# The middle pair of token tiles forms its second product by Strassen's scheme too

## The chip, the cores and the metric

The kernel runs on one core of a Trainium2 chip. The metric is the device time of one execution in microseconds (us): the median of three runs of the kernel before is 820.15 us (819.52 to 820.28). TensorE is the matrix engine, VectorE, ScalarE and GpSimd work on tiles, and SyncE (SP) only issues transfers. In the rows they are PE, DVE, ACT, POOL and SP.

## The reference

Attention within chunks of 64 tokens is followed by a feed-forward layer with softplus, all in float32:

```
scores = scale * q_c @ k_c^T        # per chunk of 64 tokens, head size 64, 8 heads, batch 8
attn   = exp(scores - max) / (sum + 1e-09)
x      = (attn @ v_c), heads side by side         # 4608 tokens x 512
h      = x @ w_in                                  # 512 -> 2048
g      = maximum(h, 0) + log1p(exp(-abs(h)))       # softplus
out    = g @ w_out                                 # 2048 -> 512, 4608 x 512
```

## The kernel before

The 4608 tokens are nine tiles of 512. Every float32 operand of the two large products is split into a high part (rounded to the type that TensorE takes) and a low part (the rest), and each product is formed by three matmuls: high by high, high by low, low by high.

The first three tiles are formed plainly (`gemm1`, `gemm2`). The other six are three pairs, and the first product of each pair (x by w_in) is formed by Strassen's scheme: seven block products in place of eight. The blocks' sums of w_in ("weight images", seven for each of eight column groups j) are made once, written to DRAM (`scratch`) and loaded again for every pair into a ring of SBUF tiles (`ring_load`, from GpSimd's queue). For each j, `product` issues seven groups of six matmuls, `hold` and `mix` combine them, `soft` applies softplus. In the first and the middle pair, the second tile's softplus results are spilled to DRAM and loaded again (`spill_store`, `spill_load`); the second product (g by w_out) is plain: `gemm2`, 12 matmuls for each of 16 chunks and each tile. In the last pair the second product is Strassen's too (`sum_product`: seven products k, eight blocks j, six matmuls each). For this its own weight images are made from w_out on VectorE and ScalarE: `v_total` (L902), `v_sum` (L915) and `v_lo` (L923), stored by `v_store` from SP's queue, half of them during the middle pair and half during the last; `image_load` (L930) brings a whole half image (1 MB). The left operand's block differences are `t_sum` (L937), and their high and low parts `g_hi` (L960) and `g_lo` (L964). `combine` (L999) adds the block results, `out_turn` (L1010) transposes them and `out_store` (L1024) writes them.

Attention for later tiles runs in bursts between the products: a burst is two halves, each 32 small matmul records for attn @ v (L661) and 32 for the scores (L557). Nine bursts lie beside the plain tiles, four beside the first pair and four beside the middle pair (three in its first product, one in its second).

The order of the work is not written by hand. Each step is a task with a cost, its needs and an urgency; `Plan.order` lists the tasks on each engine by a model of these costs, and TensorE's order is a written list (`seq`). Once listed, each engine runs its own list in order and waits on the others by semaphores; a transfer in a queue stands behind all that was issued there before. The constants at the end of the kernel (`IN_SUPER`, `QUEUE`, `V_DVE` and the like) set places, queues and engines.

Of the kernel before, what the change touches and what calls it, by code (L numbers as in the profile page):

```python
# [192 lines left out]
def chunked_attention_softplus_ffn(  # L193
# [42 lines left out]
    xpool = ctx.enter_context(tc.tile_pool(name="xpool", bufs=2))  # L236
    ld = ctx.enter_context(tc.tile_pool(name="ld", bufs=1))
# [13 lines left out]
    sp.tile([P, G_PAD], F32, name="pad", bufs=1)  # L251
# [37 lines left out]
    BOTH = (2,)  # L289
# [3 lines left out]
    def raw_tile(n, new=False):  # L293
        if new or ("raw tile", n) not in live:
            live["raw tile", n] = ld.tile([P, 2 * UW + 16], I32, name=f"raw{n}")
        return live["raw tile", n][:, : 2 * UW].bitcast(F32)
# [314 lines left out]
    def att_max(i):  # L611
        scs = live["sc", i]
        n = scs[0].shape[1]
        mx = att.tile([P, n * len(scs), scs[0].shape[2]], F32, name="mx", bufs=2)
# [23 lines left out]
    def att_den(i):  # L638
        e = live["e", i]
        den = att.tile([P, e.shape[1], e.shape[2]], F32, name="den", bufs=2)  # L640
# [99 lines left out]
    def w_image(w, k):  # L740
# [3 lines left out]
        return ring_tile(w["s"] in BOTH and w["j"] % 2, k // NX)[:, n * MT : (n + 1) * MT]  # L744

    def ring_tile(other, part):
        if other and "other" not in live:
            live["other"] = [x_tile(0, F32R) for _ in range(2)]
        t = live["other"][part] if other else x_of(FAST - 1)[part]
        return t.rearrange("p s k t -> p (s k t)")  # L750
# [42 lines left out]
    def ring_load(w, part):  # L793
        src = scratch[w["j"]]
        if w["name"] == "0_0" and part == 0:
# [3 lines left out]
        t = ring_tile(w["s"] in BOTH and w["j"] % 2, part).bitcast(F32)  # L799
        cols = slice(NX * MT, 7 * MT) if part else slice(0, NX * MT)  # L800
        on("ring").dma_start(t[:, : cols.stop - cols.start], src[:, cols])  # L801
# [50 lines left out]
    def soft(w, i, j):  # L852
        src = {(0, 0): tmp_of(0), (0, 1): tmp_of(1), (1, 0): w["bank"][0], (1, 1): tmp_of(2)}[i, j]
        if w["s"] in BOTH:
            nc.scalar.activation(u_block(w["j"], i, j), src, AF.Softplus)
            return
# [11 lines left out]
    def u_block(j, i, c):  # L868
        if ("u", j, i, c) not in live:
            n, fc = 2 * i + c, 2 * (j - 2) + i  # L870
            if j == 0:
                t = ends.bitcast(F32)[:, n * MT : (n + 1) * MT]
            elif j == 1:
                t = blk_tile(("eT", "qe")[n // 2])
            elif fc < HALF_FC:
                t = const.tile([P, DM], F32, name=("wo_hi", "wo_lo")[c] + str(fc))
            else:
                t = late_tile(2 * (fc - HALF_FC) + c, F32)
            live["u", j, i, c] = t
        return live["u", j, i, c]  # L880

    SUM_OF = (2, 3, 5, 4)

    def own_image(j, q):
        on("wo").dma_start(images[6, :, j, q, :], wo[2 * j + 1][q].bitcast(F32)[:, HC:])

    def v_space(j):
        at = SUM_AT[j]
        if ("v space", at) not in live:
            if at in SUM_RAW:  # L890
                live["v space", at] = [raw_tile(n, True) for n in range(3)]
            else:
                t = x_raw(1).rearrange("p s k t -> p (s k t)")
                live["v space", at] = [t[:, : 2 * MT], t[:, 2 * MT :]]
        return live["v space", at]

    def v_total(j, b):
        hi, lo = (t.bitcast(F32) for t in wo[2 * j + b])
        space = v_space(j)
        t = space[0]  # L900
# [3 lines left out]
    def v_sum(j, n):  # L904
        if SUM_AT[j] in SUM_RAW:
            t = v_space(j)[n // 2 - 2][:, n % 2 * MT : (n % 2 + 1) * MT]
        else:
            t = v_space(j)[n < 2][:, n % 2 * MT : (n % 2 + 1) * MT]
# [19 lines left out]
    def image_load(k, part):  # L928
        t = ring_tile(k % 2, part).bitcast(F32).rearrange("p (j q c) -> p j q c", q=2, c=HC)
        on("image").dma_start(t, images[k, :, part * FC // 4 : (part + 1) * FC // 4])  # L930

    def t_sum(n, j):
# [4 lines left out]
        (nc.gpsimd if (n, j) in TS_POOL else nc.vector).tensor_tensor(out, a, b, op=ALU.subtract)  # L937
# [4 lines left out]
    def slot_of(k, j):  # L942
        return k + 4 * (j == FC // 2 - 1) if k < 2 else (FC // 2 * k + j + 2) % GI

    def g_image(k, j):
        if ("gi", k, j) not in live:
            n = slot_of(k, j)
            if n >= GI:
                t = [w.rearrange("p a k f -> p (a k f)")[:, (n + 2) * MT : (n + 3) * MT] for w in wi[0]]
            elif k == 6:  # L950
                t = [w.rearrange("p a k f -> p (a k f)")[:, j * MT : (j + 1) * MT] for w in wi[0]]
            elif n < 2:
                t = [sp.tile([P, MT], F32R, name=f"g_{q}", bufs=LAG + 1) for q in ("hi", "lo")]
            else:
                t = [high(n - 1)[:, q * MT : (q + 1) * MT] for q in range(2)]
            live["gi", k, j] = t
        return live["gi", k, j]

    def g_hi(k, j):
        nc.scalar.copy(g_image(k, j)[0], u_block(j, *OF_G[k]))  # L960

    def g_lo(k, j):
        hi, lo = g_image(k, j)
        (nc.gpsimd if (k, j) in GL_POOL else nc.vector).tensor_tensor(  # L964
# [5 lines left out]
    def sum_product(k, j, cts, cols=slice(0, MT)):  # L970
        if k < 2 and j == 0:
            live["acc", k] = [po_tile(2 * k + ct) for ct in range(2)]
        if k > 1:
            w = ring_tile(k % 2, j // (FC // 4)).rearrange("p (j q c) -> p j q c", q=2, c=HC)[:, j % (FC // 4)]
        else:
# [762 lines left out]
```

## Time and profile before

| what | value |
|---|---|
| median of three runs | 820.15 us |
| the profiled execution, from first to last instruction | 819.6 us |
| TensorE busy | 808.6 us, 99% |
| VectorE, ScalarE, GpSimd busy | 67%, 50%, 30% |
| DMA, mean over the span | 151.27 MB, 185 GB/s |
| plain tiles, until about | 312 us |
| first pair: first product, second product | 312 to 435.8, to 484.6 us |
| middle pair: first, second | 484.6 to 608.2, to 656 us |
| last pair: first, second and end | 656 to 754, to 819.6 us |

The profile's durations overlap on TensorE: a matmul is shown from its start to its modelled end, and the next starts before. Busy shares are means over stages with different limits, so the stages are read one by one.

### The profile page before, as it was taken

How to read it: one execution, taken by the hardware profiler on the slowest of the kernel's cores; microseconds unless marked ns; L12 is line 12 of the kernel's file. 1: busy time of each engine (PE TensorE's matmuls, PEld its weight loads, DVE VectorE, ACT ScalarE, POOL GpSimd, SP SyncE). 2: the span in 40 equal slices, each digit the busy share in tenths (PEclk: the TensorE clock that was granted, in tenths of full speed). 3: DMA queues.
4: the chain of work that ended last, by engine and by line, in shares of the span. 5: the costliest groups of instructions: out<-in, count | busy, mean ns of one | idle time of the engine just before them, and what ended most of it. 6: DMA issues, size and time to landing. Idle time of an engine off the chain costs nothing.

```text
span 819.6 us, 15544 instructions
## 1 busy us (share of the span) xinstructions
PE 808.6 (99%) x5719; PEld 668.2 (82%) x5719; DVE 552.9 (67%) x1031; ACT 411.6 (50%) x694; POOL 247.8 (30%) x331
## 2 busy tenths in 40 slices
PE   9999999999999999999999999999999999999997
PEld 7878878888888888878888888888888888888885
DVE  4898985386378668355376877484766738734983
ACT  4767765345344474353445544354643455545451
POOL 1557647787887621320000000000000001000124
PEclk9999999999999999999999999999999999999999
DMA  9986758773675254986667547879775367746464
GB/s 215 250 212 182 185 169 240 217 199 94 137 194 145 49 145 158 214 207 171 210 170 223 132 115 237 255 175 253 217 225 176 116 222 234 252 169 205 126 218 69
DMA packets 200509, 151.27 MB, mean 185 GB/s; under 512 B 157520, under 2 KB 175184, under 8 KB 196208
## 3 DMA queue, kind: packets, MB, share of 16 engines
q1 hardware_dynamic: 186880, 99.89, 45.1%
q0 software_dynamic: 11680, 50.15, 20.8%
q8 instruction: 45, 0.74, 0.4%
q10 hardware_dynamic: 1872, 0.23, 0.2%
q14 instruction: 32, 0.26, 0.1%
HBM read 106.95 MB, written 41.94 MB: 182 GB/s over the span
## 4 chain that ended last, share of the span: by engine, by line
PE 85%; DVE 4%; DMA 4%; SPq 2%; issue 2%; ACT 2%; POOL 1%; POOLq 0%; DVEq 0%; ACTq 0%
PE po L1046 33%; PE pa L832 27%; PE pa L703 13%; PE po L980 8%; PE pa L661 2%; PE pa L557 2%; SPq L392 1%; DMA raw<-in_moe_w_in_dram 1%; DMA xb<-scratch 1%; PE po L413 1%; DMA late<-in_v_dram 1%; POOL out_dram L1024 1%; DVE wib L339 1%; DMA raw<-in_moe_w_out_dram 0%; DVE ka L544 0%
## 5 line engine op out<-in xcount | busy, mean ns | idle before, releaser
L1046 PE MATMUL po<-late,g_hi 128*128 128x512 f32 x420 | 128.9, 392 | 0.0
L801 POOL DMA_DIRECT2D xb<-scratch x39 | 20.9, 535 | 306.5 <-PE pa L832 279.7
L846 DVE TENSOR_TENSOR wib<-wib,pa 128x512 f32<-128x512 f32 x72 | 49.4, 687 | 71.1 <-PE pa L832 63.6
L832 PE MATMUL pa<-wi_hi,xb 128*128 128x512 f32 x304 | 93.6, 389 | 0.0
L1046 PEld LDWEIGHTS po<-late,g_hi 128*128 128x128 f32 x420 | 78.2, 188 | 16.6
L832 PE MATMUL pa<-wib,xb 128*128 128x512 f32 x360 | 87.5, 390 | 0.4 <-DVE wib L846 0.4
L1046 PE MATMUL po<-wo_hi,g_hi 128*128 128x512 f32 x224 | 84.8, 394 | 0.0
L1046 PE MATMUL po<-wo_lo,g_hi 128*128 128x512 f32 x224 | 83.8, 390 | 0.0
L1046 PE MATMUL po<-wo_hi,g_lo 128*128 128x512 f32 x224 | 83.6, 389 | 0.0
L1046 PE MATMUL po<-late,g_lo 128*128 128x512 f32 x224 | 83.3, 389 | 0.0
L832 PEld LDWEIGHTS pa<-wib,xb 128*128 128x128 f32 x360 | 67.4, 188 | 15.2 <-DVE wib L846 0.8
L715 ACT CAST g_hi<-ends 128x512 fp32r<-128x512 f32 x64 | 39.6, 619 | 78.1 <-PE po L1046 63.5
L719 DVE TENSOR_TENSOR g_lo<-ends,g_hi 128x512 fp32r<-128x512 f32 x64 | 44.0, 688 | 48.5 <-ACT g_hi L715 48.2
L711 ACT ACTIVATE u<-pa 128x512 f32<-128x512 f32 (+1 forms) x50 | 29.0, 581 | 82.1 <-PE pa L703 82.0
L838 ACT COPY wib<-pa 128x512 f32<-128x512 f32 x72 | 41.9, 588 | 50.0 <-PE pa L832 49.9
L832 PEld LDWEIGHTS pa<-wi_hi,xb 128*128 128x128 f32 x304 | 57.1, 188 | 11.8
L719 DVE TENSOR_TENSOR g_lo<-u,g_hi 128x512 fp32r<-128x512 f32 (+1 forms) x39 | 28.1, 720 | 53.4 <-ACT g_hi L715 53.1
L857 ACT ACTIVATE ends<-wib 128x512 f32<-128x512 f32 x48 | 30.3, 632 | 59.9 <-DVE wib L846 59.9
L832 PE MATMUL pa<-wi_lo,xb 128*128 128x512 f32 x152 | 59.1, 389 | 0.0
L1046 PEld LDWEIGHTS po<-wo_hi,g_lo 128*128 128x128 f32 x224 | 42.1, 188 | 9.0
L1046 PEld LDWEIGHTS po<-late,g_lo 128*128 128x128 f32 x224 | 42.0, 188 | 8.9
L1046 PEld LDWEIGHTS po<-wo_lo,g_hi 128*128 128x128 f32 x224 | 42.1, 188 | 8.6
(274 smaller groups left out, 1725.2 us busy)
## 6 DMA issues: line engine op xcount, KB each, us to landing
xb<-scratch POOLq DMA_DIRECT2D x19, 1024.0 KB, 6.0
xb<-scratch POOLq DMA_DIRECT2D x20, 768.0 KB, 6.3
raw<-in_moe_w_in_dram SPq DMA_DIRECT2D x16, 512.0 KB, 5.7
raw<-in_moe_w_out_dram SPq DMA_DIRECT2D x16, 512.0 KB, 4.9
scratch<-ends SPq DMA_DIRECT2D x16, 512.0 KB, 3.2
out_dram<-raw SPq DMA_DIRECT2D x28, 256.0 KB, 3.8
spill<-ends SPq DMA_DIRECT2D x14, 512.0 KB, 4.5
ends<-spill SPq DMA_DIRECT2D x14, 512.0 KB, 3.9
```

The lines of the kernel that those rows point to most:

```text
L557: nc.tensor.matmul(pa[c2][o, col : col + C], qT[r, a * HP + hl, :], kT[r, a * HP + hl, :], start=True, stop=True,)
L703: nc.tensor.matmul(ph, wt[:, c, :], x[:, ts_, c, :], start=(n == 0), stop=(n == 3 * KC - 1))
L711: nc.scalar.activation(w["u"], w["ph"], AF.Softplus)
L715: nc.scalar.copy(w["hi"], w["u"])
L719: (nc.gpsimd if pool else nc.vector).tensor_tensor(w["lo"], w["u"], w["hi"].bitcast(F32), op=ALU.subtract)
L801: on("ring").dma_start(t[:, : cols.stop - cols.start], src[:, cols])
L832: nc.tensor.matmul(w["bank"][BANK[k]], wts[:, q, c, :], x[:, c, :], start=k in OPENS and c + n == 0, stop=c == 1 and n == 2, skip_group_ch ...
L838: nc.scalar.copy(tmp_of(n), w["bank"][2 * (n == 2)])
L846: nc.vector.tensor_tensor(to, a, b, op=ALU.add)
L857: nc.scalar.activation(u_tiles(j)[i], src, AF.Softplus)
L980: nc.tensor.matmul(live["acc", ACC[k]][ct][:, cols], (w[:, q] if k > 1 else w[q])[:, ct * P : (ct + 1) * P], g[:, cols], start=k < 3 and j ...
L1046: nc.tensor.matmul(pos[w["m"]][t], terms[n][0][:, j * P : (j + 1) * P], terms[n][1], start=(w["first"] and n == 0), stop=n == 2 and (w["la ...
```

## The change

`BOTH`, the pairs whose second product is Strassen's, becomes `(1, 2)`. All seven weight images of w_out are now in DRAM: the four sums (`add_sums`) are made once, during the first pair, and stored from GpSimd's queue; the three that are plain parts of w_out (`own_image`) are stored beside the plain tiles and in the middle and last pair loaded again (`own_load`), since the tiles that held w_out now hold the softplus results of the pair. Images of even k are loaded one block (256 KB) at a time into tiles of their own, images of odd k by halves into the ring; the ring is loaded in four pieces per block pair instead of two in these two pairs. The last burst moves from the middle pair's second product into its first, and the four bursts of that pair are split around three matmuls. The spill of the middle pair goes away.

```
-    BOTH = (2,)
+    BOTH = (1, 2)
+    FB = BOTH[0]
...
+    def own_load(j, k):
+        on("own").dma_start(wo[FC - 4 + j % 2][k].bitcast(F32), images[k, :, j].rearrange("p q c -> p (q c)"))
+
+    def image_tile(k, j):
+        if k < 2:
+            return wo[FC - 4 + j % 2][k].rearrange("p (q c) -> p q c", q=2)
+        if k % 2:
+            return ring_tile(j // (FC // 4)).rearrange("p (j q c) -> p j q c", q=2, c=HC)[:, j % (FC // 4)]
...
+        return live["even"][j].rearrange("p (q c) -> p q c", q=2)
...
+    def image_load(k, js):
+        if len(js) == 1:
+            on("image").dma_start(image_tile(k, js[0]).bitcast(F32), images[k, :, js[0]])
+            return
...
-        (nc.gpsimd if (n, j) in TS_POOL else nc.vector).tensor_tensor(out, a, b, op=ALU.subtract)
+        (nc.gpsimd if pool else nc.vector).tensor_tensor(out, a, b, op=ALU.subtract)
...
-    IN_SUPER = ([0, 2], [0, 5], [0, 7], [1, 3])
+    IN_SUPER = ((0, 0, 2), (0, 0, 5), (0, 0, 7), (0, 1, 4), (1, 0, 1), (1, 0, 3), (1, 0, 5), (1, 0, 7))
...
-    QUEUE = dict(wd="SP", wo="SP", ring="POOL", us="SP", ul="SP", image="SP", vd="SP")
-    TS_POOL = ()
+    QUEUE = dict(wd="SP", wo="SP", ring="POOL", us="SP", ul="SP", image="SP", vd="POOL", own="SP")
...
-    V_DVE = tuple(range(8))
+    V_DVE = (0, 1, 2, 3, 4, 5, 7)
...
+    PARTS = ((0, 1, 2, 3), (4, 5, 6)), ((0, 1), (2, 3), (4, 5), (6,))
...
-            add_burst(n, 0, j)
+            if n in BOTH and (n, 0, j) in bursts:
+                for i in range(2):
+                    seq += [f"B{tag((n, 0, j))}_{i}"] + fill[i : i + 1]
+                fill = fill[2:]
+            else:
+                add_burst(n, 0, j)
...
                     pool = (t, j) in TS_POOL
-                    plan.add(f"ts{t}_{j}", "POOL" if pool else "DVE", 1.3 if pool else 0.69, partial(t_sum, t, j), needs,
+                    plan.add(f"ts{n}.{t}_{j}", "POOL" if pool else "DVE", 1.3 if pool else 0.69, partial(t_sum, t, j, pool), needs,
...
+    add_sums(FB)
     for n in BOTH:
-        add_sums(n)
+        add_second(n)
```

The new `TS_POOL` begins `((2, 2, 6), (2, 1, 0), ...` and `GL_POOL` likewise.

On TensorE, at a burst in the middle pair's first product, before (L661 and L557 are the burst's two kinds, L1046 the second product):

```order
L1046 MATMUL po_5691<-wo_hi_104,g_lo 128x512
L661 MATMUL pa<-eT,raw_5392 64x64 x16
L557 MATMUL pa<-ka,qe 64x64 x16
L661 MATMUL pa<-eT,raw_5392 64x64 x16
L557 MATMUL pa<-ka,qe 64x64 x16
L1046 MATMUL po_5688<-wo_hi_106,g_hi 128x512
L1046 MATMUL po_5688<-wo_lo_107,g_hi 128x512
```

And after (L665 and L560 are the burst, L1001 `sum_product`, L832 `product`):

```order
L1001 MATMUL po_5903<-g_hi,late_1435 128x512 x2
L1001 MATMUL po_5903<-g_lo,late_1435 128x512
L665 MATMUL pa<-eT,raw_5600 64x64 x16
L560 MATMUL pa<-ka,qe 64x64 x16
L1001 MATMUL po_5982<-g_hi,late_1436 128x512 x2
L1001 MATMUL po_5982<-g_lo,late_1436 128x512
L665 MATMUL pa<-eT,raw_5600 64x64 x16
L560 MATMUL pa<-ka,qe 64x64 x16
L1001 MATMUL po_5983<-g_hi,late_1436 128x512 x2
L1001 MATMUL po_5983<-g_lo,late_1436 128x512
L832 MATMUL pa<-wi_hi,xb 128x512 x2
```

The two halves of the burst no longer touch: three large matmuls stand between them and three behind, and then the next block pair begins.

On GpSimd, in the first pair's first product, before (L801 are the ring loads, L527 a load for attention):

```order
L801 DMA xb<-scratch 128x1536
L801 DMA xb<-scratch 128x2048
L801 DMA xb<-scratch 128x1536
L801 DMA xb<-scratch 128x2048
L801 DMA xb<-scratch 128x1536
```

And after (L930 is `v_store`, L530 a load for attention):

```order
L801 DMA xb<-scratch 128x2048
L930 DMA images<-wib_3919 128x512
L930 DMA images<-u 128x512
L801 DMA xb<-scratch 128x1536
L930 DMA images<-raw_4071 128x512 x2
L930 DMA images<-xa 128x512 x2
L801 DMA xb<-scratch 128x2048
L930 DMA images<-xa 128x512 x2
L801 DMA xb<-scratch 128x1536
L530 DMA raw_4448<-in_q_dram 32x8x32 x8
L801 DMA xb<-scratch 128x2048
```

Between most ring loads there now stand one to four stores of weight sums. Each of them waits for VectorE's last step on its tile, and the ring load waits behind it.

On VectorE, in the middle pair's second product, before (L719 are low parts, L811 and L823 the next pair's x images):

```order
L719 TENSOR_TENSOR g_lo<-ends,g_hi 128x512
L811 TENSOR_TENSOR xa<-xa 128x2x8x64
L719 TENSOR_TENSOR g_lo<-ends,g_hi 128x512
L823 TENSOR_TENSOR wi_lo<-xa,wi_hi 128x1024 x2
L719 TENSOR_TENSOR g_lo<-ends,g_hi 128x512
```

And after (L988 are low parts, L958 block differences):

```order
L988 TENSOR_TENSOR g_lo<-late_6747,g_hi 128x512
L988 TENSOR_TENSOR g_lo<-late_6837,g_hi 128x512
L958 TENSOR_TENSOR ends<-ends 128x512
L988 TENSOR_TENSOR late_1436<-ends,late_1435 128x512
L811 TENSOR_TENSOR xa<-xa 128x2x8x64
L988 TENSOR_TENSOR late_1494<-wo_end,late_1493 128x512
L988 TENSOR_TENSOR g_lo<-wo_lo_6127,g_hi 128x512
L958 TENSOR_TENSOR late_5933<-late_5933,late_5900 128x512
L823 TENSOR_TENSOR wi_lo<-xa,wi_hi 128x1024
```

Two kinds of work on the left operand stand where there was one, and the next pair's images stand among them.

## Rows read from the trace of the kernel before

**Rows 1.** Totals of the page: engine, busy us, share of the span, instructions.
```profile
PE 808.6 (99%) x5719; PEld 668.2 (82%) x5719; DVE 552.9 (67%) x1031; ACT 411.6 (50%) x694; POOL 247.8 (30%) x331
```

**Rows 2.** TensorE's waits, longest first: us in total, times, longest.
```profile
PE po L418 <- POOL ident masks.py:199: 1.4, 1, 1.4
...
PE pa L832 <- DVE wib L846: 0.4, 1, 0.4
```

**Rows 3.** Stages: length, busy us per engine, granted clock, DMA share, GB/s.
```profile
312.00:435.80 123.80, 123.36 (x897) 101.38 (x895) 68.73 (x129) 55.25 (x94) 19.82 (x34) 1.00 0.74 197
435.80:484.60 48.80, 48.80 (x333) 40.37 (x334) 39.52 (x66) 22.15 (x36) 0.00 (x0) 1.00 0.64 170
484.60:608.20 123.60, 123.60 (x901) 102.34 (x900) 83.02 (x167) 61.42 (x110) 8.50 (x16) 1.00 0.77 219
608.20:656.00 47.80, 47.80 (x271) 39.45 (x270) 33.86 (x53) 21.05 (x34) 0.53 (x1) 1.00 0.47 145
656.00:754.00 98.00, 98.00 (x435) 81.12 (x434) 53.70 (x97) 50.48 (x92) 6.90 (x13) 1.00 0.64 215
754.00:811.00 57.00, 57.00 (x253) 47.22 (x252) 47.11 (x74) 27.21 (x48) 15.51 (x24) 1.00 0.53 157
```

**Rows 4.** The chain that ended last: start, us, what.
```profile
374.29 5.44 PE pa L832 x24
...
753.93 48.97 PE po L980 x216
```

**Rows 5.** Timeline of TensorE around a joined burst: start, duration, instruction.
```profile
526.36 0.39 PE L1046 MATMUL po<-wo_hi,g_lo 128*128 128x512 f32 x1
526.68 0.69 PE L661 MATMUL pa<-eT,raw 64*64 64x64 f32 x32
...
531.62 0.62 PE L832 MATMUL pa<-wi_hi,xb 128*128 128x512 f32 x2
```

**Rows 6.** The same around a split burst (36 large matmuls in it).
```profile
117.51 2.93 PE L703 MATMUL pa<-xb,wib 128*128 128x512 f32 x12
120.36 0.69 PE L661 MATMUL pa<-eT,q 64*64 64x64 f32 x32
...
124.41 0.69 PE L661 MATMUL pa<-eT,k 64*64 64x64 f32 x32
...
128.35 0.39 PE L703 MATMUL pa<-xa,wi_hi 128*128 128x512 f32 x1
```

**Rows 7.** Groups on VectorE: busy us, mean ns of one, idle before.
```profile
L823 DVE TENSOR_TENSOR wi_lo<-xa,wi_hi 128x1024 fp32r<-128x1024 f32 x12 | 14.5, 1220 | 1.8 <-ACT wi_hi L818 1.7
L964 DVE TENSOR_TENSOR g_lo<-wo_hi,g_hi 128x512 fp32r<-128x512 f32 x12 | 8.2, 689 | 2.9 <-ACT g_hi L960 2.8
L915 DVE TENSOR_TENSOR xa<-xa 128x256 f32<-128x256 f32 x16 | 6.2, 415 | 0.1
L937 DVE TENSOR_TENSOR wo_hi<-wo_lo,wo_hi 128x512 f32<-128x512 f32 x8 | 5.5, 688 | 1.4 <-ACT wo_lo L855 1.4
L902 DVE TENSOR_TENSOR xa<-wo_hi,wo_lo 128x512 f32<-128x512 f32 x8 | 5.5, 687 | 4.5 <-DMA images<-xa 4.5
```

**Rows 8.** GpSimd's timeline: a ring load's issue in the first pair.
```profile
365.07 0.55 POOL L801 DMA_DIRECT2D xb<-scratch  x1 [10.80 <-PE pa L832]
```

**Rows 9.** All 47 ring loads, by their line.
```profile
DMA to landing us min/median/max: 4.6/5.6/8.3
```

**Rows 10.** A stretch with full DMA engines, columns as in rows 3.
```profile
326.00:350.00 24.00, 23.91 (x106) 19.50 (x105) 9.70 (x18) 9.10 (x16) 8.77 (x16) 1.00 0.92 215
```

**Rows 11.** Transfers: issuing queue, count, KB each, median us to landing.
```profile
out_dram<-raw SPq DMA_DIRECT2D x28, 256.0 KB, 3.8
...
xb<-images SPq DMA_DIRECT2D x6, 1024.0 KB, 5.0
...
k<-in_k_dram SPq DMA_DIRECT2D x96, 32.0 KB, 3.1
```

**Rows 12.** SP's timeline: eight transfers issued in a row.
```profile
377.40 3.76 SPq L527 DMA_DIRECT2D k<-in_k_dram  x8
```

More of the change, by code (lines that the diff above doesn't have):

```diff
@@ L743, in w_image, with ring_tile @@
         n = k % NX
[L744 to L750, printed above, removed]
+        return ring_tile(k // NX)[:, n * MT : (n + 1) * MT]
+    def ring_tile(part):
+        return x_of(FAST - 1)[part].rearrange("p s k t -> p (s k t)")
     def on(what):
@@ L986, in saved @@
     def saved(what, ct):
-        n = 2 * "adc".index(what) + ct
-        if "saved" not in live:
-            live["saved"] = later.tile([P, 4 * MT], F32, name="wib0")
-        return live["saved"][:, n * MT : (n + 1) * MT] if n < 4 else tmp_of(n - 4)
+        return tmp_of(2 * (what == "d") + ct)
     def set_by(what, ct):
@@ L1472, in chunked_attention_softplus_ffn @@
                 gone = [f"P{k}_{n - 1}_{FC // 2 - 1}"]
+                if n - 1 in BOTH and k == 3:
+                    gone += [f"R{n - 1}.{i}_{FC // 2 - 1}" for i in range(2)]
+                if n - 1 in BOTH and k == 2:
+                    gone += [f"R{n - 1}.2_{i}" for i in range(2)]
             needs = x_in + gone
@@ L1484, in chunked_attention_softplus_ffn @@
         d = due((n, 0, j)) - 9
-        for part in range(2):
+        parts = PARTS[n in BOTH or at > 0 and PIECES]
+        for nth, ks in enumerate(parts):
             needs = [] if at > 1 else [f"G1_{FAST * FC - 1}"]
-            if not at and not part:
+            raw = not at and not ks[0]
+            if raw:
                 needs = [f"B{BURST_AT[-1]}_{i}" for i in range(2)]
@@ L1513, in chunked_attention_softplus_ffn @@
                 take = []
-                if j > 1:
-                    needs += [f"R{i}_{j - 2}", f"vt{j - 2}_{i}"] + [f"own{j - 2}{q}" for q in range(2)] * i
+                if n > FB:
+                    needs += [f"R{n - 1}.6_{j}" + "b" * (j < SPREAD)]
                 elif j:
-                    needs += [f"B{tag(list(bursts)[-1])}_{b}" for b in range(2)]
+                    fc = u_home(j, i)
+                    needs += [f"vt{fc // 2}_{fc % 2}"] + [f"own{fc}{q}" for q in range(2)]
+                    needs += [f"G2_{v_['name']}" for w_ in pairs[at - j - FC // 2 : at - j] for v_ in w_["second"] if v_["fc"] == fc]
                 else:
@@ L1603, in add_sums @@
-                plan.add(f"ghi{k}_{j}", "ACT", 0.62, partial(g_hi, k, j), src + free, urg=d - 3 if soon else -2.5,
-                         take=[(f"gi{slot_of(k, j)}", [f"R{k}_{j}" + ("1" if k == 5 and j >= NJ - SPREAD else "")])] if k < 6 else [], after=past)
+                past = [f"{k}_{j - 1}" if j else f"{k - 1}_{NJ - 1}"] if k > 2 or k == 2 and j else [f"{i}_{NJ - 1}" for i in range(2)] if k == 2 else [f"1_{NJ - 2}"] if j == NJ - 1 else [f"{1 - k}_{j - 1 + k}"] if j + k else []
+                first = [f"ghi{n - 1}.6_{NJ - 1}"] if n > FB and not k + j else []
@@ L1605, in add_sums @@
+                plan.add(f"ghi{n}.{k}_{j}", "ACT", 0.62, partial(g_hi, k, j), src + free, urg=d - 3 if soon else -2.5,
+                         take=[(f"gi{slot_of(k, j)}", [final(n, k, j)])] if k < 6 or not j else [], after=[f"ghi{n}.{p}" for p in past] + first)
                 pool = (k, j) in GL_POOL
-                plan.add(f"glo{k}_{j}", "POOL" if pool else "DVE", 1.3 if pool else 0.69, partial(g_lo, k, j), [f"ghi{k}_{j}"], urg=-3.5 if (k, j) == (2, 0) else d - 2 if soon else -2.5)
-                part = j // (FC // 4)
```

386 lines of the change are left out of this document (216 added, 170 removed).

## The prediction

> **What bounds the kernel now.** I read the busy totals first, then TensorE's waits, then the stages, then the chain. In the totals the reader is to see that TensorE is busy for 808.6 of 819.6 us [rows 1]: hardly anything is left but the number of its matmuls. The list of its waits says where the rest lies: the longest is 1.4 us on the first constant, and of the whole pair stages only 0.4 us on VectorE appears [rows 2]. The table by stage agrees: from 312 us to 811 us TensorE's column equals the length of each stretch to within 0.5 us, at a granted clock of 1.00, the higher of the two levels (2.4 GHz), while VectorE is at 55% to 83% and the DMA engines at 0.47 to 0.77 [rows 3]. So a removed matmul is worth its full issue time, as long as the work added to the others stays hidden.
>
> What a matmul is worth is not its duration of 389 ns, since they overlap, but its spacing. In the chain 216 matmuls of the last pair's second product take 48.97 us, and 24 of a first product take 5.44 us [rows 4]: 0.2267 us each.
>
> **What it removes.** The middle pair's second product is now 32 matmul groups of 12 (16 chunks, two tiles): 384. By seven products of eight blocks it is 7 x 8 blocks x 6 = 336. That is 48 fewer, and the built order has just 48 fewer rows of that size, so the change does remove them. 48 x 0.2267 = **-10.9 us**, all on the path. With them go seven stores and loads of the spill (512 KB each) and eight evacuations; none is waited for, so I count them at nothing.
>
> **What it adds on TensorE itself.** The last four attention bursts were pairs of halves run back to back; now a half stands, three matmuls follow, then the other half. The trace has both forms. Joined: from the start of the matmul at 526.36 to the first one behind at 531.62 are 5.26 us, 13 matmuls in it are 2.95, so the burst costs 2.31 [rows 5]. Split: from 117.51 to 128.35 are 10.84 us, 36 matmuls in it are 8.16, so it costs 2.68 [rows 6]. Each change between the two tile sizes has its price, and splitting doubles their number. 4 x 0.37 = **+1.5 us**, on the path.
>
> **What it adds beside it, and whether it stays hidden.** Four covers decide.
>
> First, VectorE in the middle pair's second product. Before, that stage asked 33.9 us of 47.8 [rows 3]. Now, from the last burst to the last low part: 40 low parts at 0.689, 16 block differences at 0.688 and 5 wide operations for the next pair's images at 1.22 [rows 7], and 13 combines, turns and keeps that I take at the same 0.69: 27.6 + 11.0 + 6.1 + 9.0 = 53.7 us. TensorE needs 1.4 + 2.7 + 39 x 1.36 = 57.1 us until it wants the last of them. That is 94% filled, where the last pair, which already works this way, has 47.1 of 57.0, 83%, and TensorE never waits there [rows 3]. The lists that name differences and low parts for GpSimd hold triples, while the test asks for pairs: nothing matches, so all of it stays on VectorE, as the order shows. Bounds: nothing lost (demand below the cover), or up to 6.3 us (rival 2). It is nearer to the 83% case, so I take 0.5.
>
> Second, the first pair's first product. There the weight sums now run: 16 totals at 0.687 and, VectorE's share, 56 half-wide ones at 0.415 [rows 7], 34 us on top of 68.7 of 123.8: 83%, no limit. Their 32 stores of 256 KB move from SP's queue to GpSimd's, and GpSimd's queue also feeds the ring of weight images that TensorE multiplies by; every ring load is now behind stores that wait for VectorE. A ring load was issued at 365.07, when the fourth product of its block pair had ended, and the next block pair began at 374.29: 9.2 us of room [rows 4, 8]. Loads landed in 5.6 us at the median and 8.3 at the worst of 47 [rows 9]. The added 8.4 MB are, at the rate of the last pair's first product (215 GB/s at a share of 0.64, so 336 GB/s at a full one [rows 3]), 25 us of all engines: the share rises from 0.74 to about 0.94. A stretch of 0.92 exists, 326 to 350 us, and TensorE was busy 23.91 of its 24 us [rows 10]. Bounds: 0 to 10 us (rival 3); by the nearest row close to nothing, and I take 0.3.
>
> Third, the bank that a burst holds. Behind the second half there used to stand 12 matmuls (2.7 us) before the next first product wanted a bank; now there are 3, so 2.0 us of cover are gone, four times. Bounds 0 to 8 us; the first half's readers start earlier by a good part of that, so I take 0.1 each, 0.4.
>
> Fourth, image and own-weight loads. Even images come one block (256 KB) at a time. The first goes out once the last burst has read its tile; some 5.4 us of matmuls and burst follow before it is wanted, against 3.8 us for a 256 KB transfer in the trace [rows 11]: hidden. Later blocks are issued a whole product (10.9 us) ahead. Without this cover the price would be one landing, 3.8 us. A page of the Trainium skill speaks against these pieces: "DMA: Bandwidth & Descriptors", section "Bandwidth", asks for at least 1 MiB per DMA, and its section on the GpSimd path gives 2.0 us plus the bytes at 436 GB/s, by which 256 KB would take 2.6 us. The trace agrees in direction (1 MB in 5.0 us, a quarter of it in 3.8), not that pieces are served one by one: eight transfers leave SP within 3.76 us while each takes about 3 us to land [rows 11, 12]. By the rule alone there would be a stall (rival 4), by the rows none.
>
> **The sum.** 819.6 - 10.9 + 1.5 + (0.5 + 0.3 + 0.4) = 811.4 us of span. The median of the runs, 820.15, lies 0.55 above the profiled span, so the forecast is **812.0 us**. Head and tail of the program keep their order, the first 120 us entirely.
>
> **Rivals.**
> 1. Nothing is added: splitting costs nothing where a full-size matmul follows at once, and every cover holds: 820.15 - 10.9 = 809.3, with a little, up to 809.9. For it: TensorE's waits are nil in every covered stage. Against: the split price is measured on the same instructions.
> 2. VectorE becomes the bound in the middle pair's second product. A low part cannot start before ScalarE's copy of the same block; in one group 12 of them show 2.9 us of idle time in front, 0.24 each [rows 7]. If each of the 40 has it, VectorE needs 53.7 + 9.7 = 63.4 us against 57.1, 6.3 us late: 817.8 instead of the 0.5 taken. Against: in that same stage of the last pair this idle time is there and costs TensorE nothing.
> 3. Slower than before: the ring loads of the first pair land too late, because GpSimd's queue holds them behind stores and the DMA engines are full. Its place is the start of each of eight block pairs, its price the landing beyond 9.2 us. At a landing of 10.4 us the eight lose 9.6 us and the gain is gone; at 11 us they lose 14, and the time is 825. For it: a share of 0.94. Against: the worst landing so far is 8.3.
> 4. Small image pieces are served one by one: 8 x 3.8 = 30 us for a product of 10.9, lost three times, some 58 us: 870. The overlap in the rows all but excludes it.
>
> **How the numbers follow.** My forecast has 0.68, its own range 810.4 to 814.5 (burst price 1 to 1.5, waits 0 to 4). Rival 1 has 0.10, rival 2 0.16, rival 3 0.05, rival 4 0.01. The range that should hold 8 in 10 starts inside rival 1 and ends short of rival 2's worst: 809.4 to 817.5. About 0.2% (1.6 us) is what a measurement of this kernel can tell from no change. The forecast and rival 1 are faster; of rival 2, 0.03 reach the band around 820; rivals 3 and 4 are slower: 0.91, 0.03, 0.06.
>
> **What would show it.** In the profile after: TensorE idle under 2 us between 120 and 800 us; stage lengths of about 162 us for the middle pair (before 171) and unchanged ones for the first and the last; each of the four late bursts near 2.7 us; VectorE above 85% in the middle pair's second product with the low parts one to three blocks ahead; ring loads landing under 9 us in the first pair. Waits of TensorE on low parts there would speak for rival 2, waits on ring tiles between 312 and 440 us for rival 3. I am wrong if the middle pair shortens by less than 6 us or another stage grows by more than 2.

## The result, and the profile after

The changed kernel takes 812.99 us (median of 4 runs, 811.08 to 813.29) against 820.21 for the kernel before: a ratio of the means of 0.9908, 95% interval 0.9894 to 0.9923. A second set of runs gave 812.18 against 819.94, again 0.9908 (0.9895 to 0.9920). The forecast was 812.0 with a range of 809.4 to 817.5. Two executions of the kernel before that took 1252.8 and 2093.2 us are in none of the figures.

The page's totals after, to be set against [rows 1]: TensorE has the 48 matmuls less and VectorE 57 instructions more.

```profile
PE 799.4 (99%) x5671; PEld 659.0 (81%) x5671; DVE 590.1 (73%) x1088; ACT 425.4 (53%) x719; POOL 334.5 (41%) x477
```

The stages after, columns as in [rows 3]: first pair's first and second product, then the middle pair's, then the last pair's. TensorE fills each to within 0.1 us at a clock of 1.00. VectorE in the first pair's first product has gone from 69 to 98 us (the weight sums), and in the middle pair's second product, fourth row, from 33.9 of 47.8 to 53.0 of 59.3 us; that is fuller than the last pair's, at 43.4 of 55.6.

```profile
312.40:434.40 122.00, 121.90 (x892) 100.51 (x891) 97.65 (x201) 65.48 (x124) 40.87 (x70) 1.00 0.85 248
434.40:482.90 48.50, 48.50 (x332) 39.55 (x331) 37.36 (x63) 22.04 (x36) 19.42 (x33) 1.00 0.77 203
482.90:591.40 108.50, 108.50 (x879) 88.57 (x881) 87.16 (x167) 62.24 (x104) 24.35 (x42) 1.00 0.73 202
591.40:650.70 59.30, 59.30 (x283) 48.88 (x273) 53.01 (x79) 31.97 (x53) 17.17 (x27) 1.00 0.79 256
650.70:748.00 97.30, 97.30 (x430) 80.33 (x429) 43.62 (x63) 46.62 (x79) 21.06 (x37) 1.00 0.67 212
748.00:803.60 55.60, 55.60 (x247) 45.75 (x246) 43.41 (x69) 23.25 (x40) 15.50 (x24) 1.00 0.52 147
```

In the chain that ended last, the middle pair's plain second product stood before in these two stretches, and the last pair's in the 216 matmuls of [rows 4].

```profile
608.22 24.70 PE po L1046 x108
...
634.02 21.99 PE po L1046 x96
```

After, both pairs have a stretch of the new form (first fence below), unbroken. In the list of TensorE's waits nothing is left behind 120 us; its two longest are these, both in the head (second fence).

```profile
591.72 59.02 PE po L1001 x258
...
743.44 54.68 PE po L1001 x240
```

```profile
PE po L421 <- POOL ident masks.py:199: 1.4, 1, 1.4
PE pa L487 <- ACT late L640: 0.7, 1, 0.7
```

I take the time apart at four marks: the first matmul of each pair's first product and the last matmul of all. Two traces of either kernel (the second from the runs below):

| stretch, us | before | after |
|---|---|---|
| up to the first pair | 313.5, 313.1 | 312.2, 312.1 |
| first pair | 170.9, 170.1 | 170.6, 171.2 |
| middle pair | 171.4, 171.3 | 167.7, 167.7 |
| last pair, to the last matmul | 158.0, 158.0 | 153.0, 153.0 |
| behind the last matmul | 5.8, 5.8 | 5.7, 5.6 |

The last two pairs are the same to 0.1 us in both traces, and together they get 8.6 us shorter. What scatters lies ahead of them, but the first pair also got longer. Besides these four traces, four of the runs below (joined bursts, the same with keys from another queue, doubled low parts, VectorE relieved) have the changed kernel's first pair with the same order on every engine, and the two without 48 matmuls have that of the kernel before. It takes 170.6 to 171.7 us in six traces after (median 171.1) and 169.8 to 170.9 in four before (median 170.1), so about 1.0 us more. 8.6 less 1.0 is 7.6; the medians of the two sets of runs give 7.2 and 7.8. The gain of the last two pairs is shared between the two because the kernel before pushed two chunks of the middle pair's second product, 24 matmuls or 5.4 us, behind the start of the last pair; now nothing is pushed. Adding up the distances between the starts of successive matmuls, from the middle pair's first to the last, there are 1418 distances behind large matmuls before and 1370 after; those behind the small ones of the bursts add up to 7.24 us before and 7.80 after.

### The profile page after: what moved, and what is told of

Read it like the earlier page. It is cut to its first block, busy times and chain, and to the rows that moved or that the text cites. A ratio compares the mean times of both kernels' runs of the same rounds, so it can differ in the third digit from the quotient of the medians.

```text
span 809.3 us, 15889 instructions
## 1 busy us (share of the span) xinstructions
PE 799.4 (99%) x5671; PEld 659.0 (81%) x5671; DVE 590.1 (73%) x1088; ACT 425.4 (53%) x719; POOL 334.5 (41%) x477
## 4 chain that ended last, share of the span: by engine, by line
PE 92%; DVE 4%; DMA 1%; issue 1%; ACT 1%; POOL 1%; SPq 0%; POOLq 0%; DVEq 0%; ACTq 0%
PE pa L832 27%; PE po L1066 25%; PE po L1001 18%; PE pa L707 14%; PE pa L665 2%; PE pa L560 2%; PE po L416 1%; PE po L421 1%; DMA eT<-ka 1%; DVE wib L342 1%; DMA raw<-in_moe_w_in_dram 1%; PE po L461 1%; PE po L633 0%; DVE ka L547 0%; DVE g_lo L723 0%
## 5 line engine op out<-in xcount | busy, mean ns | idle before, releaser
L801 POOL DMA_DIRECT2D xb<-scratch x79 | 43.0, 545 | 220.4 <-PE pa L832 198.2
L832 PE MATMUL pa<-wi_hi,xb 128*128 128x512 f32 x368 | 113.4, 389 | 0.0
L832 PE MATMUL pa<-wib,xb 128*128 128x512 f32 x432 | 105.5, 390 | 0.1
L832 PEld LDWEIGHTS pa<-wib,xb 128*128 128x128 f32 x432 | 80.9, 188 | 17.5 <-DVE wib L846 0.5
L846 DVE TENSOR_TENSOR wib<-wib,pa 128x512 f32<-128x512 f32 x72 | 49.5, 687 | 57.8 <-PE pa L832 49.0
L1066 PE MATMUL po<-late,g_hi 128*128 128x512 f32 x300 | 91.0, 392 | 0.0
L832 PEld LDWEIGHTS pa<-wi_hi,xb 128*128 128x128 f32 x368 | 69.1, 188 | 14.4
L1044 POOL DMA_DIRECT2D out_dram<-raw x48 | 31.1, 656 | 106.9 <-DVE raw L1028 105.2
L832 PE MATMUL pa<-wi_lo,xb 128*128 128x512 f32 x184 | 71.6, 389 | 0.0
L1066 PE MATMUL po<-wo_hi,g_hi 128*128 128x512 f32 x160 | 59.6, 395 | 0.0
L1066 PE MATMUL po<-wo_lo,g_hi 128*128 128x512 f32 x160 | 58.8, 390 | 0.0
L1066 PE MATMUL po<-late,g_lo 128*128 128x512 f32 x160 | 58.4, 389 | 0.0
L584 DVE STREAM_TRANSPOSE eT<-qe 32x256 f32<-32x256 f32 x104 | 45.2, 434 | 3.2 <-POOL qe L652 1.8
L707 PE MATMUL pa<-xb,wib 128*128 128x512 f32 x192 | 46.2, 389 | 0.3 <-DVE qe L627 0.3
L707 PEld LDWEIGHTS pa<-xb,wib 128*128 128x128 f32 x192 | 36.0, 188 | 8.1 <-POOL wib L364 0.7
L832 PEld LDWEIGHTS pa<-wi_lo,xb 128*128 128x128 f32 x184 | 34.5, 188 | 7.3
L707 PE MATMUL pa<-xb,wi_hi 128*128 128x512 f32 (+1 forms) x144 | 39.3, 368 | 0.4 <-DVE xb L686 0.2
```

The source lines that it names most:

```text
L584: nc.vector.transpose(live["eT", i][d : d + BL, tb], e[s : s + BL, kb])
L707: nc.tensor.matmul(ph, wt[:, c, :], x[:, ts_, c, :], start=(n == 0), stop=(n == 3 * KC - 1))
L801: on("ring").dma_start(t[:, n * MT : (n + len(ks)) * MT], src[:, ks[0] * MT : (ks[-1] + 1) * MT])
L832: nc.tensor.matmul(w["bank"][BANK[k]], wts[:, q, c, :], x[:, c, :], start=k in OPENS and c + n == 0, stop=c == 1 and n == 2, skip_group_ch ...
L846: nc.vector.tensor_tensor(to, a, b, op=ALU.add)
L1044: eng.dma_start(out[r0 : r0 + rows, c0 : c0 + BL].rearrange("(b t) d -> t b d", t=BL), t.rearrange("t (b d) -> t b d", d=BL))
```

## Experiments

Each kernel is told by its edit, with what was on record before it ran. "Trace" means from the start of the middle pair's first matmul to the start of the last of all (329.0 us before, 320.4 after; the table above goes to its end, 0.3 us later) unless another stretch is named.

**The changed kernel and the kernel before once more.** No edit.

> The changed kernel as it is, timed on the same chip as the three that follow and as the kernel before. Theory (matmuls saved, burst price, hardly any wait): span 809.3 to 811.5 us, time 811 to 813.3, 0.9908 of the kernel before within 0.0015. Rival (the profiled span of 809.3 was the usual one and the other three were disturbed by 2 us): the times gather at 811.1 and the ratio at 0.989.

> The kernel before, once more, for a second trace of it: how much of the 819.6 us of its first profile belongs to stretches that the change doesn't touch. Theory (from the middle pair's start to the last matmul the kernel before always takes 329.4 us, and what scatters is the stretch ahead of it): 329.2 to 329.6 us there, and a span of 817.5 to 819.2. Rival (the stretch itself scatters): 328 or less there.

Measured: 812.18 us (811.48 to 813.81) and 820.33. The trace was 320.44 us again after, and 329.01 before, where the first one had 329.09; to the end of the last matmul, as the expectation has it, it was 329.3, inside its range. Both theories hold, but for one execution after at 812.0 us of span, 0.5 above its range. The spans of eight executions after lie between 809.3 and 812.0, with 810.95 in the middle; of the 49 executions of the kernel before that ran beside the experiments 818.4 is the middle. So the profiled execution of the kernel before, 819.6, stands in the upper part, and the first one after, 809.3, is the shortest of its eight: between these two profiles lie 10.3 us, between the middles 7.4.

**Joined bursts.** Undoes one part: both halves of a late burst run back to back.

```
-                for i in range(2):
-                    seq += [f"B{tag((n, 0, j))}_{i}"] + fill[i : i + 1]
-                fill = fill[2:]
+                add_burst(n, 0, j)
```

> The changed kernel with its four late bursts joined again: both halves run back to back, the two halves of the second-product block behind them. Theory (each split adds two changes of tile size, 0.33 to 0.37 us a burst): 1.3 to 1.5 us shorter than the changed kernel, and each joined burst costs about 2.3 us. Rival (the split is there because a joined burst must wait for accumulator banks): not shorter, or longer by 1 to 4 us, with TensorE waiting ahead of the bursts' second halves or ahead of the next first product.

Measured: 812.59 us, ratio to before 0.9906 (0.9892 to 0.9920); trace 320.37, 0.07 less than with split bursts. Both theories were half right. The joined bursts cost less, but two of the four then wait inside. TensorE's waits in this stretch (us in total, times, longest):

```profile
PE pa L560 <- DVE ka L537: 0.9, 2, 0.6
```

L560 is the scores of the second half, L537 the transposition of its keys. The wait is on keys, not on an accumulator bank: in the chain of waits stands the load of the keys, which SP's queue had issued late (5.5 to 5.9 us for the 8 transfers of one block).

**Joined bursts, and keys from another queue.** The same, and two key loads on GpSimd's queue.

```
-    ON_POOL = (..., ('q', 34), ('k', 20))
+    ON_POOL = (..., ('q', 34), ('k', 20), ('k', 33), ('k', 35))
```

> The changed kernel with its late bursts joined, as in the run above with joined bursts, and two of the loads of keys (8 transfers each) moved from SP's to GpSimd's queue, since the joined bursts' second halves waited 0.7 and 0.4 us for keys that SP's queue had issued late. Theory (joining saves 0.33 us a full burst and the waits came from SP's queue): from the middle pair's start to the last matmul 1.2 to 1.5 us less than the 320.4 of the changed kernel. Rival (the keys land too late from GpSimd's queue as well, or ring loads behind them do): no shorter, with the waits still there or moved to ring tiles.

Measured: 810.96 us (809.89 to 811.66), ratio 0.9879 (0.9854 to 0.9905); trace 319.12, 1.32 less than the changed kernel, as the first theory had it. A joined burst in it, timeline of TensorE (start, duration, instruction): the four groups of 64x64 matmuls follow each other with no gap.

```profile
536.87 0.69 PE L665 MATMUL pa<-eT,raw 64*64 64x64 f32 x32
537.38 0.65 PE L560 MATMUL pa<-ka,qe 64*64 64x64 f32 x32
537.85 0.67 PE L665 MATMUL pa<-eT,raw 64*64 64x64 f32 x32
538.32 0.67 PE L560 MATMUL pa<-ka,qe 64*64 64x64 f32 x32
538.92 0.73 PE L1001 MATMUL po<-g_hi,late 128*128 128x512 f32 x2
```

And the second half of the same burst when split, in the changed kernel:

```profile
537.61 0.40 PE L1001 MATMUL po<-g_lo,late 128*128 128x512 f32 x1
537.93 0.69 PE L665 MATMUL pa<-eT,raw 64*64 64x64 f32 x32
538.45 0.65 PE L560 MATMUL pa<-ka,qe 64*64 64x64 f32 x32
539.02 0.72 PE L1001 MATMUL po<-g_hi,late 128*128 128x512 f32 x2
```

From the last large matmul to the first small one pass 0.32 us instead of 0.227, some 0.09 more for the change of tile size. On the way back the step from the last small matmul to the first large one takes 0.148 where small ones follow each other in 0.016 on average, some 0.13 more, and the first distance of the large ones is longer by 0.11. These three make the 0.33 us that a split costs. [Rows 5] and [rows 6] showed the same two forms before. This is the fastest kernel of the study by its median; its interval and that of the changed kernel overlap, so the trace carries the 1.3 us, not the times.

**48 matmuls less, in two places of the kernel before.** The same line in `gemm2`, for the first or the second tile of the middle pair.

```
+            if n == 2 and w["m"] == SUPERS[1] and 2 <= w["fc"] < 14:        # the first run
+            if n == 2 and w["m"] == SUPERS[1] + 1 and 1 <= w["fc"] < 13:    # the second
+                continue
```

> The kernel before with nothing changed but 48 matmuls left out: in 12 of the 16 chunks of the first tile of the middle pair, the third of the three terms of the second product (4 matmuls each) is not multiplied, so these outputs lack a correction. Theory (TensorE is the bound there and a matmul is worth its spacing of 0.2267 us): 10.9 us shorter than the kernel before, 808.7 us of span. Rival (the stage is held by the spill's loads or by VectorE's low parts once TensorE is faster): 6 us shorter or less, with waits of TensorE in the middle pair's second product.

> The kernel before with 48 matmuls left out in another place than in the run above that left out 48: here it is the third of the three terms in 12 chunks of the second tile of the middle pair, whose second product runs by itself at the pair's end, not between the first products (these outputs lack a correction). Theory (there TensorE alone is the bound; the run above lost part of its gain to ring loads and hold copies, which had been hidden under the matmuls between the first products): 10.9 us shorter than the kernel before in the trace, and 10 to 11 in the times. Rival (VectorE's low parts or the spill's loads decide once TensorE needs less): 6 us or less, with TensorE waiting on them.

Measured: the first 814.55 us against 819.94, 5.4 less (ratio 0.9926, 0.9911 to 0.9942); the second 811.08 against 820.49, 9.4 less (0.9890, 0.9875 to 0.9906). Traces 323.4 and 320.4. The first tile's chunks stand between the products of the middle pair's first product; with four matmuls less in each, TensorE waits there:

```profile
PE pa L832 <- ACT wib L838: 2.0, 1, 2.0
PE pa L832 <- DMA xb<-scratch: 1.9, 2, 1.1
```

The second run has one wait of any size, where the last pair begins:

```profile
PE pa L832 <- ACT wib L838: 1.4, 1, 1.4
PE po L1048 <- ACT g_hi L715: 0.2, 1, 0.2
```

So in the traces the saved matmuls were worth 10.9 us less what the covers then lacked: 2.3 us in the second run, 5.2 in the first. The rival of the first run (covers decide) was right in size, but not in place: TensorE waited in the first product, and neither the spill's loads nor VectorE's low parts were named. The theory of the second fell short, with 8.6 us in the trace and 9.4 in the times; 1.4 us went to a wait that I had not named.

**More work for VectorE.** 24 of the 40 low parts of the middle pair's second product are made twice.

```
+        if n_ == 1 and 3 <= k <= 5:
+            nc.vector.tensor_tensor(lo, u_block(j, *OF_G[k]), hi.bitcast(F32), op=ALU.subtract)
```

> The changed kernel with 24 more VectorE operations in the middle pair's second product: each low part of its products 3 to 5 (counted from 0) is computed twice, with the same result. Theory A (VectorE has room there as the trace after shows: operations follow each other at 0.605 us, not at their duration of 0.69, so 24 cost 14.5 us; 2.8 us of idle time in that stretch and a lead of about 3.5 us are used up first): 8 us longer than the changed kernel, between 6 and 10. Theory B (the prediction's own arithmetic, by durations: 53.7 + 16.6 us against 57.1): 13 us longer. Rival C (VectorE is far from the bound): under 3 us longer.

Measured: 825.16 us, 13 more than the changed kernel; trace 331.97, 11.5 more. TensorE's waits in that stretch, and VectorE's column (the third), at 46.9 of 48.0 us:

```profile
PE po L1003 <- DVE g_lo L992: 3.3, 4, 1.0
PE po L1003 <- DVE late L992: 2.4, 5, 0.8
PE po L1003 <- DMA qe<-images: 2.0, 1, 2.0
```

```profile
600.00:648.00 48.00, 41.11 (x168) 30.27 (x167) 46.92 (x72) 22.65 (x39) 6.47 (x11) 1.00 0.54 189
```

Neither price was right. In VectorE's timeline of the changed kernel operations of 0.69 us start 0.60 us apart; a repeat that writes the tile just written starts 0.72 behind (612.46 to 613.17 in the second fence):

```profile
596.52 0.69 DVE L988 TENSOR_TENSOR late<-wo_hi,late 128x512 fp32r<-128x512 f32 x1
597.12 0.68 DVE L1017 TENSOR_TENSOR wib<-wib,po 128x512 f32<-128x512 f32 x1
597.72 0.69 DVE L988 TENSOR_TENSOR late<-wo_hi,late 128x512 fp32r<-128x512 f32 x1
```

```profile
612.46 0.68 DVE L988 TENSOR_TENSOR late<-wo_hi,late 128x512 fp32r<-128x512 f32 x1
613.17 0.69 DVE L992 TENSOR_TENSOR late<-wo_hi,late 128x512 fp32r<-128x512 f32 x1
613.79 0.69 DVE L988 TENSOR_TENSOR late<-wo_hi,late 128x512 fp32r<-128x512 f32 x1
```

24 x 0.72 = 17.3 us were asked and 11.5 lost, so the stage had 5.8 us of VectorE to give. That agrees with the 5.7 us of idle time between its operations in the trace after, from 591.7 us to the end of the last low part. In this run the chain that ended last stays on VectorE from 612 to 649 us, and the wait of 2.0 us that is put down to an image load ended together with a low part.

**VectorE relieved.** The lists of triples are put to use.

```
-                    pool = (t, j) in TS_POOL
+                    pool = (n, t, j) in TS_POOL
...
-                pool = (k, j) in GL_POOL
+                pool = (n, k, j) in GL_POOL
```

> The changed kernel with the two lists of triples put to use: 26 block differences and 38 low parts of the last two pairs go to GpSimd (1.3 us each in the planner's table) instead of VectorE. Theory (VectorE is not the bound, TensorE never waits for it in these stages): no gain, between 0.5 us shorter and 4 us longer than the changed kernel; longer if a ring load stands behind one of the slower operations on GpSimd. Rival (VectorE at 90% costs some of the time by contention or late low parts): 1 us shorter or more.

Measured: 835.54 us, 23 more than the changed kernel; trace 342.4, 22 more. No gain, as the theory had it, but a loss far beyond the 4 us it allowed. GpSimd takes 1.31 us for a low part, VectorE 0.69, and TensorE now waits for GpSimd. But GpSimd is not full: from 595 to 669 us it is busy for 41 of 74 us. Before the low part that TensorE waited longest for, it had itself waited 8.7 us for VectorE's work on the next pair's images (L811). So engines waited for each other in the order of their lists; another order was not tried. Waits in the last two pairs, then GpSimd's row with that wait at its end, then four stretches of 4 us (columns as above; the clock is the last but two):

```profile
PE po L1001 <- POOL late L988: 9.7, 3, 5.9
PE po L1001 <- POOL g_lo L988: 2.6, 1, 2.6
```

```profile
L988 POOL TENSOR_TENSOR late<-ends,late 128x512 fp32r<-128x512 f32 x2 | 2.6, 1285 | 8.7 <-DVE xa L811 8.7
```

```profile
608.00:612.00 4.00, 3.54 (x16) 2.54 (x14) 3.82 (x4) 1.65 (x4) 0.00 (x0) 1.00 1.02 355
612.00:616.00 4.00, 0.00 (x0) 0.00 (x0) 3.50 (x3) 1.48 (x2) 0.00 (x0) 0.76 0.85 324
616.00:620.00 4.00, 2.54 (x6) 1.82 (x6) 2.92 (x3) 1.04 (x1) 1.26 (x1) 0.50 0.00 2
...
628.00:632.00 4.00, 4.00 (x19) 3.31 (x18) 3.54 (x5) 0.00 (x0) 0.97 (x2) 1.00 0.48 125
```

**The stores of the weight sums, three ways.** From SP's queue; twice to the same place; a second copy to another place.

```
-        on("vd").dma_start(images[SUM_OF[n], :, j], live["vs", j, n])
+        nc.sync.dma_start(images[SUM_OF[n], :, j], live["vs", j, n])       # from SP's queue
...
+        for _ in range(2):                                                  # the same place
+            on("vd").dma_start(images[SUM_OF[n], :, j], live["vs", j, n])
...
+        on("vd").dma_start(spare[j][n], live["vs", j, n])                   # another place, as well
```

> The changed kernel with the 32 stores of weight sums issued from SP's queue, as in the kernel before, at the same places of the program's order. Theory (GpSimd's queue has room for them, TensorE never waits on a ring tile in the first pair): the first pair within 0.5 us of its 171 us, or up to 3 us longer where SP's loads of queries, keys and values stand behind a store that waits for VectorE. Rival (the stores on GpSimd's queue cost the first pair something): 0.5 us shorter or more.

> The changed kernel with each of the 32 stores of weight sums in the first pair done twice, to the same place: 8.4 MB more through GpSimd's queue between 312 and 435 us, where the DMA engines' share is 0.85. At the full rate of about 336 GB/s they are 25 us of all engines, 0.20 of this stretch: 1.05 in all. Theory (rival 3 of the prediction is real, but its point lies beyond the change): ring loads land after their 9.2 us of room, TensorE waits on them, and the first pair takes 3 to 10 us longer. Rival (stores and the queue's order never delay a ring load, the share is no measure of room): under 1 us longer.

> The changed kernel with the second copy of each weight-sum store going to a place of its own in DRAM, which nobody reads: the same 8.4 MB more in the first pair, the same 32 more issues on GpSimd's queue, but no store that has to wait until its twin has landed. Theory (what cost 80 us when both copies went to one place was the waiting at the head of GpSimd's queue, in front of the ring loads, not the bytes): the first pair returns to within 1 to 8 us of its 171 us, the share of the DMA engines there rises from 0.85 to near 0.95 or more. Rival (the bytes or the number of issues in that queue are what counts): the first pair stays 30 us or more longer.

Measured: from SP's queue 813.13 us, the first pair 171.9, no gain. Twice to the same place 892.54 us, the first pair 250.9, 80 us more, far beyond the theory; and the share of the DMA engines fell to between 0.63 and 0.67. Some 65 of the 80 us are gaps between large matmuls, some 15 are large matmuls 0.427 us apart at the lower clock (0.87 in the mean of this first pair). The reason for the gaps is GpSimd's own waits between 312 and 500 us: a second copy is not issued before the first has landed, and the ring loads stand behind it. TensorE's waits are below them.

```profile
POOL images L931 <- DMA images<-xa: 54.6, 14, 6.8
...
POOL images L931 <- DMA images<-raw: 16.0, 5, 5.2
```

```profile
PE pa L832 <- DMA xb<-scratch: 43.4, 7, 10.9
PE po L1067 <- ACT raw L1074: 10.6, 1, 10.6
```

With the copy to another place, 825.78 us (821.14 to 829.35), the first pair 185.0: 13 to 14 us more. Most of the 80 was the waiting, as the theory said, but the loss is above the 8 it allowed. The share of the DMA engines in the first product is 0.90. Ring loads of 1 MB now land in 8.6 us (6.5 in the changed kernel); of the stores, those from the tiles `xa` land in 9.3 (5.6), all first copies in 7.7 (6.9). TensorE's waits in the first product name not the ring but ScalarE's copy of a held product, which stands in ScalarE's order among the weight sums' copies:

```profile
PE pa L833 <- ACT wib L839: 6.4, 1, 6.4
PE pa L833 <- DVE wib L847: 2.0, 1, 2.0
```

```profile
xb<-scratch POOLq DMA_DIRECT2D x6, 1024.0 KB, 8.6
...
images<-xa POOLq DMA_DIRECT2D x15, 256.0 KB, 9.3
```

What makes that copy late, and whether the bytes or the 32 issues do it, I did not separate.

**Large ring pieces.** Two loads a block pair in the last two pairs, 1 MB and 768 KB. The planner's order changes a little with it, TensorE's does not.

```
-    PARTS = ((0, 1, 2, 3), (4, 5, 6)), ((0, 1), (2, 3), (4, 5), (6,))
+    PARTS = ((0, 1, 2, 3), (4, 5, 6)), ((0, 1, 2, 3), (4, 5, 6))
```

> The changed kernel with the ring loads of the middle and the last pair in two pieces a block pair (1 MB and 768 KB) as in the first pair, instead of three of 512 KB and one of 256 KB; the same bytes. A piece of four products can only be asked for when the fourth of them is done. Theory (what counts is the room ahead of a load, not its size): from there to the next block pair are three products and what stands behind them, 6.8 us, against a landing of 6.6 us at the median for 1 MB: TensorE waits 0 to 2 us in most of the 16 block pairs, 4 to 12 us in all, and the waits are named on ring tiles. Rival, by the rule of the Trainium skill (DMA: Bandwidth & Descriptors, section Bandwidth: at least 1 MiB per DMA): no longer than the changed kernel, perhaps shorter.

Measured: 821.46 us, 1.0013 of the kernel before (1.0000 to 1.0025): the whole gain is gone. Trace 327.1, 6.6 us more, as the theory's 4 to 12 had it. But TensorE waits on ring tiles in two places, not in most of the 16 block pairs, for 3.6 us in the first of these rows; 1.3 us are waits for VectorE, and the rest lies in smaller delays. What the times lose beyond the 6.6 lies in the stretch ahead: the first pair of this trace takes 172.4 us.

```profile
PE pa L832 <- DMA xb<-scratch: 3.6, 2, 2.1
PE pa L832 <- DVE wib L846: 1.1, 1, 1.1
```

In the middle pair's first product the 1 MB pieces landed in 5.9 us, the changed kernel's 512 KB in 5.0 (medians). The larger piece has the better rate and the later end, and its request must wait for four products where the smaller one waits for two. The Trainium skill's rule (DMA: Bandwidth & Descriptors, section Bandwidth: at least 1 MiB) is about rate; here rate was not what TensorE waited for.

## Why the prediction was right, and where it was off

**The matmuls.** 48 x 0.2267 = 10.9 us on the path: right. The large matmuls fell by 48, and no wait took their place. The two runs without 48 matmuls show that this needed the rest of the change: taken out of the kernel before, they give back 2.3 and 5.2 us, much of it to late copies and ring loads. In the changed kernel these waits are absent; that the smaller ring pieces have a part in it is shown by the run with large ones, that the new order has one is not shown.

**The bursts.** +1.5 by splitting: measured 1.32 for the four, by joining them with the keys in time. All of it lies at the edges, where the tile size changes. The Trainium skill (TensorEngine Tiling (Array Packing), section Key Properties) says that changing the tiling mode drains TensorE. The trace fits this, with some 0.09 us going in and 0.13 and 0.11 coming out, though no row shows a drain as such. What the prediction missed is that splitting also hides late keys, so undoing it alone gains nothing.

**VectorE in the middle pair's second product, +0.5, and rival 2.** No wait was found there. The working by durations was too pessimistic: 53.7 of 57.1 us left 3.4 of room, the run with doubled low parts measured 5.8. Rival 2's idle time in front of the low parts is 2.4 us in all here, not 9.7, and TensorE waits for none of it. The lists did match nothing, as foretold; used, they cost 22 us.

**The first pair, +0.3, and rival 3.** This term was too small: the first pair takes about 1.0 us more, by the ten traces above. Ring loads landed in 6.5 and 6.9 us (medians of the 1 MB and 768 KB pieces), within the 9.2 of room, and the share of the DMA engines rose to 0.85, not to 0.94. One delay of 0.25 to 0.26 us, between 428 and 430 us, stands in all six traces after and in none of the four before. The chain there runs through VectorE, where a mix (L846) that TensorE's product needs stands behind two weight sums (L919) and two transpositions for attention between them:

```profile
425.82 0.42 DVE wib L919
...
427.39 0.74 DVE u L919
428.13 0.61 DVE wib L846
...
428.79 1.66 PE pa L832 x6
```

So VectorE, whose 83% the prediction called no limit, delays TensorE at this place; the trace has it at 97.7 of 122.0 us, 80%. For the rest, distances longer by up to 0.5 us between 443 and 457, the cause stays open. At the edge the prediction's mechanism is half right: with 8.4 MB more, ring loads were not what TensorE named, and the loss was 14 us; with a wait at the head of GpSimd's queue ring loads were what it named, 43.4 us of them, and the loss was 80.

**The bank held by a burst, +0.4.** Not there: in every split burst the next large matmul follows without a wait. The joined bursts waited on keys, not on banks.

**Image and own loads, hidden.** Right: no wait of TensorE names them in the changed kernel. The section on the GpSimd path that the prediction works 2.6 us out from is about transfers that GpSimd issues, while these leave SP's queue. Nor does the rule of 1 MiB say that small pieces are served one by one, so rival 4's stall did not follow from it.

**The stretch from the middle pair on.** 10.9 less 1.5, 0.5 and 0.4 is 8.5; measured 8.6. That the sum fits is partly luck. The two waits, 0.9 together, are not there; in their place stand 1.0 us (10.9 less 1.3 less 8.6) in many small delays that no list of waits names. The rows of the result show much of it: 258 and 240 matmuls of the new form take 59.02 and 54.68 us, 0.5 and 0.3 more than at 0.2267 each, 0.1 of it at the edge of the last burst. Why they are slower stays open. The sentence on the stages was wrong in its shares: the middle pair is not at 162 us but at 167.7, and the last pair is not unchanged but 4.9 shorter, since the 24 matmuls that were left over into the last pair are gone too. I had taken the stage's end from the rows, not from the order. By the prediction's own last sign, a middle pair shorter by less than 6 us, it was wrong: the middle pair is 3.7 shorter. The time came out inside the range all the same, since the other 4.9 lie in the last pair.

**The level.** Two errors cancel, which is luck. The profiled span of 819.6 was 1.2 above the middle of the kernel before, and I took 0.55 us around the span where a timed execution has 1.8. The forecast's gain of 8.2 stands against 7.2 and 7.8 in the two sets.

## What to carry to other kernels

A saved matmul is worth its spacing only where the work beside it still fits in the shorter time; look at what each wait-free stage would wait for next before counting it. When a tile is wanted at a fixed time, ask when its load can be requested and when it lands, not only at what rate it comes: here pieces of 1 MB and 768 KB lost what pieces of 512 KB had won. A sum that fits does not show that its terms do; take the stretch apart before believing it. When a split or a detour looks like a pure cost, ask what it hides: here joining the bursts paid only after the load that they would have waited for had been moved to another queue.

## What the runs showed of the hardware that was not expected

TensorE's granted clock fell after some of its waits. In the run with GpSimd's low parts it waited 5.9 us up to 617.5; the stretch from 616 to 620 shows a clock of 0.50 (1.2 GHz), with large matmuls 0.427 us apart. It waited again, 3.6 us up to 624.0, and the clock was 0.57 in the mean from 624 to 628 and 1.00 (2.4 GHz) from 628. With the second copy to another place, a wait of 6.4 us up to 396.8 was followed by a clock of 0.53 up to 400.

The length of a wait alone does not tell. Waits of 2.0, 2.1 and 2.6 us, in the runs with doubled low parts, with large ring pieces and with GpSimd's low parts, left the clock at 1.00. With the second copy to another place, a wait of 2.0 us up to 439.6 was followed by 0.50 from 440.8 to 444.2.

So a wait can cost more than itself: in the first pair of the run with the second copy to the same place some 15 of 80 us are large matmuls at the lower clock, and with the copy to another place some 2.6 of 14.
